# A two-layer attention and MLP training step on one core: the backward weight phases as steps with a look-ahead of two, the K4 rows loaded late, and weight-gradient stores moved to another queue

## The chip, the cores and the metric

One core of one Trainium2 chip runs the whole program. The metric is the device time of one execution in microseconds (us). The kernel before was run five times; its median is 1452.07 us, and all times lie between 1444.59 and 1456.94 us.

## The reference

The program computes a decode step of two layers, each used twice with the same weights, and all gradients:

```python
x = x + A(layernorm(x))   # attention over a K/V cache: B=2, 32 heads, 4 kv heads, Sk=16384, Dh=128
x = x + B(layernorm(x))   # layernorm again, w1 (1024x3584), gelu, w2 (3584x1024)
x = x + A(layernorm(x))
x = x + B(layernorm(x))
# outputs: x, and the gradients of A_x, k_cache, v_cache, wq, wo, w1, b1, w2, b2 for grad_out
```

There is one query row for each of two batch elements. The large arrays are the caches K and V (33.5 MB each, bf16), their gradients of the same size, and four weight matrices of 7 to 8 MB with their gradients. The gradients of K and V and of the weights sum over both uses of the layers.

## The kernel before, in words

The work runs in stages, one after the other, in one program that a tile scheduler orders for each engine. An engine then works strictly in that order.

**Forward** (`attn_fwd`, `mlp_fwd`, twice). K and V are streamed in tiles of 2 MB (`st`, a pool `stream` of six buffers that also serves all weights and the gradient tiles `stV`, `stK`). All loads are issued by SyncE (SP).

**Backward weight phases.** The gradient of a row vector through a weight matrix W needs W transposed. Three such phases form a chain: w2 (L580 transposes, L593 matmuls into `dh_acc`), the derivative of gelu, w1 (L647, L659, `dz_acc`), two layernorm derivatives (`ln_bwd_cols`, L473 to L485), wo (L698, L709, `do_acc`). After the attention pass comes wq (L886, L898, `dy_acc`). Each is a loop of steps: up to 16 transposes of 128x128 into two PSUM tiles `tp` (four slots), an eviction by ScalarE (L147) and one by VectorE (L149) into the pool `ktp` (four buffers), and four matmuls. `Skew` issues the transposes of step k+1 ahead of the matmuls of step k. The bank with the sums is copied by ScalarE (L529, L539), transposed on TensorE (L532, L542), and leads to the vector of the next phase. w1, wq and wo do this twice, for two halves, each half with a `Skew` of its own.

**Rows for the weight gradients.** Each weight gradient is a sum of four outer products. Their vectors are kept as rows of one tile `K4`, with rows 32j to 32j+3 for weight j. `k4_fill_T` transposes a vector, copies it, and writes it to K4 by two GpSimd DMAs (L519). `save_rows4` does so for the gradient at the start of a phase: eight transposes (L492), a ScalarE copy `r_bf` (L494), two DMAs (L524).

**Rows for attention** (`attn_bwd_pre`, L717 on): for each batch element three f32 transposes, a copy to SBUF (L726), a GpSimd DMA that moves the 32 rows to the partitions where they are used (L728), and then a product with its row sum (L730) and eight masked copies (L733, L734).

**Passes over the cache** (`bwd_pass`). Each has 16 units (2 batch elements by 8). A unit loads a V tile and a K tile, transposes V (L804), multiplies (`sc`, L816), forms `DS` (L820), transposes it (L838) into `DST`, and adds to `dq_ps` (L847), this last part one unit late. The first pass does only this and is called the half pass here. The second, the full pass, also makes the V gradient (`blkV`, L780) and the K gradient (`blkK`, L788), which ScalarE and VectorE evict (L758, L760) into `stV` and `stK`, stored by GpSimd. In between, `fill` takes blocks of a generator `wgrad_gen`: one block is one matmul of 512 columns with 32 rows of K4 (L972, `wgblk`) and one eviction (L138 or L140) into a tile `wg_st` of four blocks (a pool of three). Full tiles are stored in turn by GpSimd and by SP (L980). The full pass has 16 x (8+3) = 176 places for blocks, and w2, w1 and wo have 56 + 56 + 64 = 176 blocks.

**The tail**: wq with its 64 weight-gradient blocks and the small outputs. There, two ScalarE copies `ob` and `rb` (L494) come last.

The order of the stages: forward, chain 1 (w2, w1, wo), half pass, chain 2 (wq, w2, w1, wo), full pass, tail.

Of the kernel before, what the change touches and what calls it, by code (L numbers as in the profile page):

```python
# [9 lines left out]
BF16 = mybir.dt.bfloat16  # L10
# [39 lines left out]

class KB:
    def __init__(self, ctx, tc, aps, debug=None):
# [30 lines left out]
        self.ktp = self.es_main.enter_context(tc.tile_pool(name="ktp", bufs=4))  # L83
# [328 lines left out]
    def mlp_fwd(self, l, x_in):  # L412
# [25 lines left out]
        sq = self.small.tile([P, FT, NB], F32, name="g_sq")  # L438
        nc.vector.tensor_tensor(out=sq[:], in0=hp[:], in1=hp[:], op=ALU.mult)
        inner = self.small.tile([P, FT, NB], F32, name="g_inner")  # L440
        nc.vector.tensor_scalar(inner[:], sq[:], GA, 1.0, op0=ALU.mult, op1=ALU.add)
        arg = self.small.tile([P, FT, NB], F32, name="g_arg")
# [3 lines left out]
        hh = self.small.tile([P, FT, NB], F32, name="g_hh")  # L446
# [40 lines left out]

    def cols_to_rows_bf(self, colsT_bf, name):
# [4 lines left out]
        r = self.small.tile([NB, D], BF16, name=name, tag="rowbf2", bufs=2)  # L493
# [5 lines left out]
    def k4_slot(self, w, which, l, b):  # L499
        j, na, nb = self.K4_LAYOUT[w]  # L500
        r = 32 * j + 2 * l + b
        if which == "A":
            return self.K4[r:r + 1, 0:na]
        return self.K4[r:r + 1, na:na + nb]

    def k4_fill_T(self, w, which, l, src_cols, n2, blk):
        nc = self.nc
        ps = self.tp_tile([n2, P], BF16, name="k4ps")
        nc.tensor.transpose(ps[:], src_cols, self.ident[:])
        sb = self.small.tile([64, P], BF16, name="k4sb")  # L510
# [10 lines left out]
    def save_rows4(self, w, which, l, colsT_bf):  # L521
        r = self.cols_to_rows_bf(colsT_bf, "r4_bf")
# [3 lines left out]
    def extract_streams(self, acc_bank, nblk, dst_fn, name):  # L526
        nc = self.nc
        asb = self.kt_tile([P, 512], name=name + "_sb")
# [7 lines left out]
    def extract_sum(self, acc_bank, dst, name):  # L536
        nc = self.nc
        asb = self.kt_tile([P, 512], name=name + "_sb")
# [6 lines left out]
    def mlp_bwd(self, l, S, dxT, reuse_w2=False):  # L545
        nc = self.nc
        W = self.W
        dmT = self.small.tile([P, 8, NB], BF16, name="dmT")
        nc.vector.tensor_copy(dmT[:], dxT[:])
        self.save_rows4("w2", "B", l, dmT)  # L550
        if l == 1:
            nc.vector.tensor_copy(W["dxsum"][:], dxT[:])
        else:
            nc.vector.tensor_tensor(out=W["dxsum"][:], in0=W["dxsum"][:], in1=dxT[:], op=ALU.add)
        dhT = self.small.tile([P, FT, NB], F32, name="dhT")
        CH = 7
        wts = []
        for q in range(4):
            if reuse_w2:
                wts.append(S["w2tiles"][q])  # L560
            else:
                wt = self.stream_tile([P, CH, D])
                nc.sync.dma_start(wt[:], self.w2_v[:, q * CH:(q + 1) * CH, :])
                wts.append(wt)
# [526 lines left out]
```

## Time and profile before

| | |
|---|---|
| median of five runs | 1452.07 us |
| the profiled execution | 1456.94 us, of which the span is 1455.2 us |
| mean granted TensorE clock | 0.878 |
| TensorE busy | 1154.6 us (79%) |
| VectorE, ScalarE, GpSimd busy | 690.0, 553.5, 70.2 us |
| bytes moved by DMA | 488.01 MB, mean 335 GB/s |

The profile is taken from one execution. Its page gives the busy time of the engines, a row of 40 slices, the queues, the chain that ended last and the costliest groups; further views of the trace give each instruction with its start, its length and, in brackets, the idle time of its engine ahead of it with what ended that. L numbers are lines of the kernel before. "SPq" is SyncE's queue of DMA issues.

### The profile page before, as it was taken

The page shows a single profiled execution, that of the slowest core. Times are in us where ns is not written, and L with a number is a line of the kernel's source. Part 1 is how long each engine was busy: PE and PEld are TensorE (multiplying, and loading weights), DVE is VectorE, ACT ScalarE, POOL GpSimd, SP SyncE. Part 2 cuts the span into 40 slices and gives each one's busy share as a digit, 9 for nine tenths or more (in the row PEclk, how much of TensorE's full clock was granted, in tenths as well). Part 3 has the DMA queues.
Part 4 walks back from the last instruction along what each step waited for, and adds up shares of the span by engine and source line. Part 5 has one row for each costly group of instructions (what it writes and reads, how often), then busy time and mean ns, then how long its engine had stood idle before and what let it go on. Part 6 is the DMA issues. An engine that isn't in the chain of part 4 may idle for free. (4 is left out here: it accounts for less than half of the span.)

```text
span 1455.2 us, 32908 instructions
## 1 busy us (share of the span) xinstructions
PE 1154.6 (79%) x14512; PEld 699.0 (48%) x14576; DVE 690.0 (47%) x1242; ACT 553.5 (38%) x930; POOL 70.2 (5%) x120
## 2 busy tenths in 40 slices
PE   3998556589963678769987878779989999989685
PEld 2665433356653346546655556554444444433243
DVE  2566002145530224445544443457766767666553
ACT  1454000045520005422211125436657666666455
POOL 1000000000000000000000000001101001101000
PEclk9999767789975779889998888899999999998866
DMA  9998999997899983958998773917999999999963
GB/s 379 408 355 322 389 396 405 412 398 301 316 346 406 404 309 141 336 215 331 379 368 319 303 271 143 373 62 295 419 386 409 390 411 396 376 413 352 390 241 149
DMA packets 127817, 488.01 MB, mean 335 GB/s; under 512 B 5362, under 2 KB 5616, under 8 KB 122554
## 3 DMA queue, kind: packets, MB, share of 16 engines
q1 hardware_dynamic: 105642, 402.17, 71.4%
q0 software_dynamic: 22032, 83.73, 14.2%
q8 instruction: 114, 1.87, 0.5%
q14 instruction: 29, 0.24, 0.0%
HBM read 386.94 MB, written 98.58 MB: 334 GB/s over the span
## 5 line engine op out<-in xcount | busy, mean ns | idle before, releaser
L804 PE MATMUL tp<-ident,st 128*128 128x128 bf16 x2048 | 172.1, 229 | 23.0 <-DVE rows L726 13.2
L804 PEld LDWEIGHTS <-st 128*128 128x128 bf16 x2048 | 137.5, 103 | 80.0 <-issue 42.9
L246 PEld LDWEIGHTS <-st 128*128 128x128 bf16 x2048 | 119.4, 100 | 75.5 <-issue 60.7
L246 PE MATMUL tp<-ident,st 128*128 128x128 bf16 x2048 | 143.9, 224 | 12.4 <-DMA st<-in_A_k_cache_dram 12.1
L147 ACT COPY vT<-tp 128x512 f32<-128x512 f32 x128 | 75.3, 588 | 202.7 <-PE tp L804 202.6
L816 PE MATMUL sc<-vT,DOPB 128*128 128x512 bf16 x448 | 142.8, 389 | 5.8 <-DVE DS L820 3.9
L149 DVE COPY vT<-tp 128x1024 bf16<-128x1024 bf16 x128 | 88.3, 690 | 115.5 <-PE tp L804 114.1
L147 ACT COPY kT<-tp 128x512 f32<-128x512 f32 x128 | 74.8, 584 | 170.4 <-PE tp L246 169.4
L149 DVE COPY kT<-tp 128x1024 bf16<-128x1024 bf16 x128 | 87.6, 689 | 92.0 <-PE tp L246 91.0
L758 ACT CAST stV<-blkV 128x512 bf16<-128x512 f32 x160 | 92.2, 589 | 49.5 <-PE blkV L780 48.0
L788 PE MATMUL blkK<-QRP,DS 128*128 128x512 bf16 x256 | 87.0, 404 | 24.2 <-ACT stK L758 9.7
L327 PE MATMUL osc<-st,PT 128*8 128x128 bf16 x2048 | 54.4, 293 | 62.5 <-DMA st<-in_A_v_cache_dram 46.4
L758 ACT CAST stK<-blkK 128x512 bf16<-128x512 f32 x160 | 88.8, 587 | 39.8 <-PE blkK L788 39.8
L140 DVE CAST wg_st<-wgblk 128x512 bf16<-128x512 f32 x120 | 82.1, 687 | 37.1 <-PE wgblk L972 32.6
L820 DVE SCALAR_TENSOR_TENSOR DS<-sc,delta,PALL 64x1024 bf16<-64x1024 f32 (+1 forms) x64 | 82.3, 1286 | 33.6 <-PE sc L816 33.6
L972 PE MATMUL wgblk<-K 32*128 32x512 bf16 x240 | 92.8, 423 | 5.9 <-ACT wg_st L138 4.5
L261 PE MATMUL sc<-kT,QP 128*32 128x512 bf16 x512 | 88.0, 388 | 5.9 <-ACT kT L147 3.5
L760 DVE CAST stK<-blkK 128x512 bf16<-128x512 f32 x96 | 65.2, 690 | 44.6 <-PE blkK L788 44.2
L780 PE MATMUL blkV<-DORP,PALL 128*128 128x512 bf16 x256 | 84.1, 385 | 1.8 <-issue 0.2
L138 ACT CAST wg_st<-wgblk 128x512 bf16<-128x512 f32 x120 | 70.3, 589 | 36.4 <-PE wgblk L972 22.3
L327 PEld LDWEIGHTS <-PT 128*8 128x8 bf16 x2048 | 48.9, 118 | 66.9 <-issue 66.2
L847 PE MATMUL dq_ps<-st,DST 128*8 128x128 bf16 x2048 | 69.0, 227 | 6.3 <-DVE DST L149 5.1
(259 smaller groups left out, 1330.0 us busy)
## 6 DMA issues: line engine op xcount, KB each, us to landing
st<-in_A_k_cache_dram SPq DMA_DIRECT2D x64, 2048.0 KB, 16.3
st<-in_A_v_cache_dram SPq DMA_DIRECT2D x64, 2048.0 KB, 12.1
st<-in_B_w_dram SPq DMA_DIRECT2D x28, 1792.0 KB, 18.2
st<-in_A_wq_dram SPq DMA_DIRECT2D x16, 2048.0 KB, 11.7
st<-in_A_wo_dram SPq DMA_DIRECT2D x16, 2048.0 KB, 19.9
out_dram<-stV POOLq DMA_DIRECT2D x16, 2048.0 KB, 16.0
out_dram<-stK POOLq DMA_DIRECT2D x16, 2048.0 KB, 16.0
out_dram<-wg_st POOLq DMA_DIRECT2D x23, 512.0 KB, 10.9
```

The lines of the kernel that those rows point to most:

```text
L147: nc.scalar.copy(o.bitcast(F32), i.bitcast(F32))
L149: nc.vector.tensor_copy(o, i)
L246: nc.tensor.transpose(tp[:, gi, tt, :], kts[b][:, 2 * gp + gi, 4 * tg + tt, :], self.ident[:])
L261: nc.tensor.matmul(sc2[RB:RB + 32, tgi, :], lhsT=QP[:, b, g, :], rhs=kTs[b][:, gi, :, :], start=(g == 0), stop=(g == G - 1), tile_position ...
L327: nc.tensor.matmul(osc[32 * g:32 * g + 8, b, 0:DH], lhsT=PT[:, t, 32 * b + 8 * g:32 * b + 8 * g + 8], rhs=vts[b][:, g, t, :], start=(u == ...
L758: nc.scalar.copy(out, in_)
L780: nc.tensor.matmul(blk[:, :], lhsT=self.PALL[:, c0:c0 + P], rhs=W["DORP"][:, b, :, :], start=True, stop=True)
L788: nc.tensor.matmul(blk[:, :], lhsT=DS[:, t_ * P:(t_ + 1) * P], rhs=W["QRP"][:, b, :, :], start=True, stop=True)
L804: nc.tensor.transpose(tp[:, gi, tt, :], vt[:, 2 * gp + gi, 4 * tg + tt, :], self.ident[:])
L816: nc.tensor.matmul(sc2[:, tgi, :], lhsT=DOPB[:, b, g, :], rhs=vT[:, gi, :, :], start=(g == 0), stop=(g == G - 1))
L820: nc.vector.scalar_tensor_tensor(DS[ra, m * 1024:(m + 1) * 1024], sc2[ra, :, :].rearrange("p a b -> p (a b)"), W["delta"][ra, 0:1], self.P ...
L972: nc.tensor.matmul(blk[:, :], lhsT=self.K4[32 * j:32 * j + 32, ib * P:(ib + 1) * P], rhs=self.K4[32 * j:32 * j + 32, na + cg:na + cg + 512 ...
```

## The change

1. Each backward weight phase becomes an object `Phase`, with `prologue` (its loads and the transposes of the first two steps), `run` (transposes of step k+2 ahead of the matmuls of step k) and `epilogue` (the sums out). `run_bwd_chain` strings phases together: the prologue of the next phase is issued ahead of the epilogue of this one. The two halves of w1, wq and wo are one sequence of steps. The pool `ktp` has six buffers instead of four. The copies of the sums have a tile of their own, `xsb`, with one buffer.
2. The two layernorm derivatives after w1 become one function, `ln2_bwd_cols`, with one reduction over the partitions instead of two.
3. `save_rows4` and `k4_fill_T` only note what is to be written (the first copies a 128x16 vector). `k4_load` writes all rows of one weight when its blocks begin. K4 is allocated and zeroed late, all weights use rows 0 to 3, and a block multiplies all 128 rows. After each load the generator gives away 12 places (4 for wq) without a block.
4. `attn_rows` casts to bf16 and transposes straight to the partitions where the rows are used; the copy and the DMA in between are gone.
5. In the full pass the sums into `dq_ps` come in the same unit.
6. Every second weight-gradient store is issued by ScalarE instead of SP.
7. Several small tiles have one buffer, among them the tile of `ob` and `rb`.

```diff
-        self.ktp = self.es_main.enter_context(tc.tile_pool(name="ktp", bufs=4))
+        self.ktp = self.es_main.enter_context(tc.tile_pool(name="ktp", bufs=6))
...
+class Phase:
...
+    def prologue(self, n):
+        for f in self.pre:
+            f()
+        self.n = max(1, min(n, len(self.steps)))
+        for k in range(self.n):
+            self.steps[k][0]()
+
+    def run(self):
+        n = self.n
+        assert n >= 1
+        for k in range(len(self.steps)):
+            if k + n < len(self.steps):
+                self.steps[k + n][0]()
+            self.steps[k][1]()
...
+        def finish(ph):
+            ph.run()
+            start(nxt[id(ph)])
+            ph.epilogue()
...
+    def save_rows4(self, w, which, l, colsT_bf):
+        keep = self.persist.tile([P, 8, NB], BF16, name=f"k4keep_{w}{l}")
+        self.nc.vector.tensor_copy(keep[:], colsT_bf[:])
+        self.k4_src.setdefault(w, []).append(("R", w, which, l, keep))
...
-        r = self.small.tile([NB, D], BF16, name=name, tag="rowbf2", bufs=2)
+        r = self.small.tile([NB, D], BF16, name=name, tag="rowbf2", bufs=1)
...
-            ps = self.tp_tile([32, 3, DH], F32, name="rows_ps")
-            nc.tensor.transpose(ps[:, 0, :], dOT[:, :, b], self.identf[:])
...
-            r0 = self.small.tile([32, 3, DH], F32, name="rows0", bufs=1)
-            nc.vector.tensor_copy(r0[:], ps[:])
+            ps = self.tp_tile([P, 3, DH], BF16, name="rows_ps")
+            for k in range(3):
+                nc.tensor.transpose(ps[rs, k, :], srcb[:, k, b, :], self.ident[:], tile_position=(0, RB))
             rows = self.small.tile([P, 3, DH], F32, name="rowsRB", bufs=1)
-            nc.gpsimd.dma_start(rows[rs, :, :], r0[:])
+            nc.vector.tensor_copy(rows[rs, :, :], ps[rs, :, :])
...
-                pend["dq"] = dq_fn
                 if mode == 4:
+                    dq_fn()
...
+            self.k4_load(w)
+            for _ in range(idle_after_load):
+                yield
...
-                        nc.tensor.matmul(blk[:, :], lhsT=self.K4[32 * j:32 * j + 32, ib * P:(ib + 1) * P],
-                                         rhs=self.K4[32 * j:32 * j + 32, na + cg:na + cg + 512],
-                                         start=True, stop=True, tile_position=(32 * j, 0))
+                        nc.tensor.matmul(blk[:, :], lhsT=self.K4[:, ib * P:(ib + 1) * P],
+                                         rhs=self.K4[:, na + cg:na + cg + 512], start=True, stop=True)
...
-                (nc.gpsimd if qctr[0] % 2 == 0 else nc.sync).dma_start(dst, src)
+                (nc.gpsimd if qctr[0] % 2 == 0 else nc.scalar).dma_start(dst, src)
```

What the scheduler makes of it, at three places. First ScalarE in chain 1, from the last copy of w1's sums to wo; `dz_acc` and `do_acc` are the banks of w1 and wo, `w1T` (now `dzT`) and `woT` the evicted transposes. Before:

```order
L147 COPY w1T<-tp 128x512 x7
L539 CAST dz_sb<-dz_acc 128x512
L494 COPY r_bf<-c2r_ps 2x8x128
L147 COPY woT<-tp 128x512 x8
L529 CAST do_sb<-do_acc 128x512
```

And now:

```order
L175 COPY dzT<-tp 128x512 x7
L612 CAST xsb<-dz_acc 128x512
L175 COPY woT<-tp 128x512 x9
L602 CAST xsb<-do_acc 128x512
L175 COPY woT<-tp 128x512 x7
```

The copy `r_bf` between the sums of w1 and the first transposes of wo is gone, and the first half of wo is left one eviction later, since the second half has begun.

Second TensorE in the seventh unit of the half pass, around the transposes of `DS` (tiles with their buffer numbers, the same `DS` tile in all rows of a fence). Before, the seam ahead of the first eight transposes and the one between the two groups of eight:

```order
L847 MATMUL dq_ps_9162<-st_10082,DST_10273 8x128
L838 LDWEIGHTS DS_10275
...
L838 MATMUL tp_10452<-ident_82,DS_10275 128x32
L804 LDWEIGHTS st_10472
```

And now, the seam between the two groups and the one behind the second:

```order
L957 MATMUL tp_10370<-ident_82,DS_10193 128x32
L935 LDWEIGHTS DOPB3_9066
L935 MATMUL sc2_10274<-vT_10299,DOPB3_9066 128x512
...
L957 MATMUL tp_10370<-ident_82,DS_10193 128x32
L966 LDWEIGHTS DST_10387
L966 MATMUL dq_ps_9080<-st_10196,DST_10387 8x128
```

The sums into `dq_ps` of the unit before stood ahead of the transposes of `DS`, and next V's transposes behind; now the sums stand behind, and use the `DST` that has just been made. Units 2 to 8 have the first form before, units 2 to 5 now; units 9 and 11 to 16 have the second form in both.

Third ScalarE at the end of the full pass, from the last K blocks on (`dyT`, before `wqT`, are transposes of wq). Before:

```order
L758 CAST stK<-blkK 128x4x128 x10
L138 CAST wg_st<-wgblk 128x512
L147 COPY wqT<-tp 128x512 x8
L539 CAST dy_sb<-dy_acc 128x512
L138 CAST wg_st<-wgblk 128x512 x27
```

And now:

```order
L877 CAST stK<-blkK 128x4x128 x10
L166 CAST wg_st<-wgblk 128x512 x4
L1136 DMA out_dram<-wg_st 128x2x1024
L166 CAST wg_st<-wgblk 128x512 x3
L1136 DMA out_dram<-wg_st 128x2x1024
L166 CAST wg_st<-wgblk 128x512 x5
```

Between the last K block and the first transposes of wq, 39 blocks of the gradient of wo now stand in a row on TensorE; before there were 3.

More of the change, by code (lines that the diff above doesn't have):

```diff
@@ L500, in k4_slot @@
         j, na, nb = self.K4_LAYOUT[w]
[L501 removed]
+        r = 2 * l + b
         if which == "A":
@@ new lines, in epi, with dst_fn @@
+        def epi():
+            dhT = self.small.tile([P, FT, NB], F32, name="dhT")
+            acc = st["acc"]
+            accf = acc[:, :, :].rearrange("p a c -> p (a c)")
+            for half in range(2):
+                f0, nf = (0, 4) if half == 0 else (4, 3)
+                def dst_fn(k, src, f0=f0):
+                    nc.vector.tensor_copy(dhT[:, f0 + k:f0 + k + 22:7, :], src)
+                self.extract_streams(acc[:, 0, :] if half == 0 else accf[:, 512:1024], nf, dst_fn, "dh")
+            box["dhT"] = dhT
```

459 lines of the change are left out of this document (279 added, 180 removed).

## The prediction

> **What bounds the kernel now.** I first cut the execution into its stages: columns are the stretch, its length, the busy time of TensorE (PE), its weight loads, VectorE, ScalarE and GpSimd with counts, the granted TensorE clock, the DMA share and the rate.
>
> ```profile
> 0.00:538.00 538.00, 380.05 (x6137) 254.50 (x6137) 182.80 (x367) 125.03 (x216) 16.96 (x38) 0.84 0.96 375
> 538.00:642.60 104.60, 78.65 (x946) 57.86 (x947) 44.08 (x123) 41.02 (x54) 3.56 (x7) 0.86 0.63 239
> 642.60:840.00 197.40, 168.47 (x2528) 114.77 (x2559) 95.61 (x127) 37.52 (x64) 0.51 (x1) 0.92 0.83 321
> 840.00:972.70 132.70, 104.29 (x1272) 76.14 (x1273) 58.29 (x151) 51.57 (x72) 4.52 (x9) 0.87 0.60 223
> 972.70:1382.00 409.30, 369.06 (x3219) 166.67 (x3250) 273.55 (x413) 260.34 (x472) 39.83 (x56) 0.95 0.95 376
> 1382.00:1455.20 73.20, 54.05 (x412) 29.02 (x411) 35.70 (x63) 38.05 (x52) 4.79 (x9) 0.69 0.49 196
> ```
>
> The rows are forward, chain 1, half pass, chain 2, full pass, tail. Forward has its DMA engines busy for 0.96 of the time; without the K4 transposes its TensorE order is the same as before, so I leave its 538 us. The chains and the tail leave the DMA engines idle for 0.37 to 0.51 of their time: there TensorE and the waits on the way from one weight to the next set the time. The full pass has both near their limits.
>
> Then the TensorE timeline of chain 1 (start, length, what; in brackets its idle time before and what ended it).
>
> ```profile
> 540.60 1.01 PE L190 MATMUL r2c_ps<-identf,gr 2*128 2x2 f32 x8 [5.76 <-DVE gr L160]
> ...
> 555.35 1.19 PE L580 MATMUL tp<-ident,st 128*128 128x128 bf16 x16
> ...
> 557.96 1.22 PE L580 MATMUL tp<-ident,st 128*128 128x128 bf16 x16
> ...
> 568.73 0.41 PE L593 MATMUL dh_acc<-w2T,dmT 128*2 128x384 bf16 x4 [0.25 <-ACT w2T L586]
> ...
> 571.74 1.96 PE L647 MATMUL tp<-ident,st 128*128 128x128 bf16 x32
> ...
> 590.88 1.23 PE L659 MATMUL dz_acc<-w1T,dhpT 128*2 128x512 bf16 x8
> ...
> 604.68 1.02 PE L709 MATMUL do_acc<-woT,daT 128*2 128x512 bf16 x4
> ...
> 607.93 1.21 PE L698 MATMUL tp<-ident,st 128*128 128x128 bf16 x16
> ...
> 609.60 1.22 PE L698 MATMUL tp<-ident,st 128*128 128x128 bf16 x16
> ...
> 616.60 0.59 PE L709 MATMUL do_acc<-woT,daT 128*2 128x512 bf16 x3 [0.17 <-DVE woT L149]
> ...
> 642.62 1.87 PE L804 MATMUL tp<-ident,st 128*128 128x128 bf16 x16 [8.47 <-DVE rows L726]
> ```
>
> In the loops TensorE is dense: two steps of w2 take 557.96 - 555.35 = 2.61 us, one step of wo 609.60 - 607.93 = 1.67 us. The seams are not: from the end of w1 (592.11) to the first sum of wo (604.68) pass 12.6 us, and at the end of wo 8.47 us go by before the cache pass starts. Two rows say why, one of ScalarE and one of VectorE; with them two groups of the page (busy time, mean ns of one) that price an eviction of 512 columns:
>
> ```profile
> 598.88 4.80 ACT L494 COPY r_bf<-c2r_ps 2x1024 bf16<-2x1024 bf16 x1 [6.10 <-PE c2r_ps L492]
> 640.13 0.28 DVE L730 SCALAR_TENSOR_TENSOR dl_junk<-rowsRB 32x128 f32<-32x128 f32 x1 [5.72 <-DMA rowsRB<-rows]
> ```
>
> ```profile
> L140 DVE CAST wg_st<-wgblk 128x512 bf16<-128x512 f32 x120 | 82.1, 687 | 37.1 <-PE wgblk L972 32.6 <-ACT stV L758 3.7 <-PE blkV L780 0.6
> L138 ACT CAST wg_st<-wgblk 128x512 bf16<-128x512 f32 x120 | 70.3, 589 | 36.4 <-PE wgblk L972 22.3 <-DMA out_dram<-wg_st 12.9
> ```
>
> A 4.80 us copy on two partitions stands ahead of ScalarE's evictions, and VectorE waits 5.72 us for a DMA. An eviction takes 0.59 us on ScalarE and 0.69 on VectorE.
>
> **Chain 1, part by part.** Start: w2's first transposes stood behind the row copy of the gradient (`r2c_ps` is the last matmul ahead of it, and ends at 541.6); now nothing is between. Eight pairs of 2.61 make 20.9 us; with 2 us that I allow for a cold start they end at 541.6 + 22.9 = 564.5 instead of 569.1: **-4.6**. K4's clearing now stands on ScalarE ahead of the first eviction, where `r_bf` stood; the four PSUM tiles hide it, or it costs at most what that copy takes, 4.80.
>
> w1 to wo: five steps of transposes (80, by the order) now stand ahead of the first sum, where there were two. Half a phase of eight steps takes 8 x 1.67 = 13.4 us, plus 0.8 for the sums' transposes and the reduction: TensorE could end it at 592.1 + 14.2 = 606.3. The dependent chain I put at 7.3 us: the copy 0.6, 32 transposes ahead of its own 2.4, one eviction on VectorE 0.7, and some fourteen short VectorE operations, one reduction fewer than before, 3.6 at about 0.26 (the row L730 is 0.28). It ends at 599.4, after which 3 steps of transposes and 8 of sums, 8.2 us, remain: 607.6 against 617.2, **-9.6**. If the evictions hold up VectorE, up to half is lost.
>
> Attention rows: the DMA wait of 5.72 us goes; three casts come, 0.84 at 0.28. Next late is VectorE's masked copying of the first batch element, which the second's copy waits for. **-4.9**, between -3 and -5.7. Of the small seams the longest is from w2 to w1, 569.14 to 571.74, 2.6 us; with the middles of w1 and wo I take half of that and 0.75 each: **-2.8**, between 0 and -7.8. Sum **-22**.
>
> **Half pass.** Its code is the same, but the order isn't (the second place above). The loads of K on SP, one per unit, give the two paces:
>
> ```profile
> 674.02 0.37 SPq L772 DMA_DIRECT2D st<-in_A_k_cache_dram  x1
> ...
> 684.85 0.37 SPq L772 DMA_DIRECT2D st<-in_A_k_cache_dram  x1
> ...
> 778.72 0.37 SPq L772 DMA_DIRECT2D st<-in_A_k_cache_dram  x1
> ...
> 792.27 0.37 SPq L772 DMA_DIRECT2D st<-in_A_k_cache_dram  x1
> ```
>
> A unit of the first form takes 10.83 us, one of the second 13.55. Units 6, 7 and 8 change from the first to the second form: 3 x 2.72 = 8.2, and unit 10 loses some 0.8. **+9**; 0 if the transfers set the pace there, which the DMA share of 0.83 over the stage speaks against.
>
> **Chain 2.** The same rows, with wq ahead of w2:
>
> ```profile
> 843.74 3.59 PE L886 MATMUL tp<-ident,st 128*128 128x128 bf16 x32
> ...
> 868.51 1.24 PE L898 MATMUL dy_acc<-wqT,DQTb 128*2 128x512 bf16 x8
> ...
> 902.37 0.39 PE L593 MATMUL dh_acc<-w2T,dmT 128*2 128x384 bf16 x4 [0.27 <-ACT w2T L586]
> ...
> 972.70 1.86 PE L804 MATMUL tp<-ident,st 128*128 128x128 bf16 x16 [4.78 <-DVE rows L726]
> ```
>
> From the end of wq (869.75) w2 needs 20.9 + 0.8 us, and some 2 us of waits stay: 893.5 instead of 902.8, **-9.2**. w1 to wo again **-9.6**, the attention rows **-1.2** (the idle time is 4.78 here, 3.7 less than in chain 1), the first 32 transposes of wq, now ahead of the wait for their input, **-3.5**, the small seams **-2.8**. Sum **-26**.
>
> **Full pass.** SP now has only loads. Before, a store in its queue that waits for VectorE held the loads behind it:
>
> ```profile
> SPq L980 <- DVE wg_st L140: 360.9, 27, 27.8
> ```
>
> But what could earlier loads bring? The middle of the pass, from the fourth unit's first V transpose to the fifteenth's, eleven units, and the third's start:
>
> ```profile
> 1045.80:1323.10 277.30, 254.16 (x2216) 114.72 (x2239) 186.60 (x275) 179.48 (x326) 26.70 (x38) 0.96 1.01 399
> 1022.50 0.89 PE tp L804 x16
> 1045.80 1.00 PE tp L804 x16
> 1377.05 0.39 PE L788 MATMUL blkK<-QRP,DS 128*128 128x512 bf16 x1
> ```
>
> A unit without transfer waits takes 1045.8 - 1022.5 = 23.3 us, the mean is 277.3/11 = 25.2, and the DMA engines are full at 399 GB/s. So the loads there were late because the engines were full. The start and the end can gain: from 972.7 to the last K block at 1377.4 are 404.7 us. The bytes up to there, at 2.1 MB a tile and 0.13 MB a block, are 14 pairs of loads (58.7), 31 stores (65), 137 blocks (18) and two tiles of wq (4.2): 146 MB, at 400 GB/s 365 us, behind some 15 us in which the first V gradient is made. By TensorE it is 16 x 23.3 less 39 blocks moved out, 0.32 each by the two evictions side by side: 360, plus some 15 us for rows, transposes and bunched blocks after each K4 load. Both come to 375 to 380; two limits so near each other cost some more: 385, **-20** (0 to -29).
>
> [...]
>
> Widening a block from 32 to 128 rows of K4 I put at nothing: 512 columns stream either way; the DMA of the rows is covered by the 12 places given away (over a unit), or costs a landing three times, at most the 10.9 us each of the store row below.
>
> **The tail.** The 39 blocks now stand between the pass and wq:
>
> ```profile
> out_dram<-wg_st POOLq DMA_DIRECT2D x23, 512.0 KB, 10.9
> 1346.08 21.80 DMA out_dram<-wg_st
> 1395.74 12.47 PE L972 MATMUL wgblk<-K 32*128 32x512 bf16 x32
> 1413.43 0.82 PE L886 MATMUL tp<-ident,st 128*128 128x128 bf16 x6 [2.60 <-DMA st<-in_A_wq_dram]
> 1445.80 5.01 ACT L494 COPY rb<-c2r_ps 2x1024 bf16<-2x1024 bf16 x1
> ```
>
> By the evictions 39 blocks take 39 x 0.32 = 12.5 us. But they fill ten tiles of a pool of three, and a store lands 10.9 us after its issue (median; 21.80 once): about 7/3 rounds of 10.9, **25 us**. What follows shortens: wq's start is hoisted (-3.5 as in chain 2), the wait of 2.60 goes, 64 blocks can go at 0.32 instead of the 12.47/32 = 0.39 us of the row (-4.5), and with one sequence for both halves I take -5.5 of the 73.20 - 54.05 = 19 us in which TensorE idles in the tail. With one buffer, `rb` waits for the store of `ob`: `rb` ends at 1450.8, and its own store and the program's end take the 4.4 us behind it, so 0 to 4.4; I take +2.4. Net 25 - 3.5 - 2.6 - 10 + 2.4 = **+11**, between -2 and +36.
>
> **Sum.** -22 + 9 - 26 - 20 + 11 = -48. The profiled execution took 1456.94, so 1409; the median of the runs is 4.9 lower: **1404 us**.
>
> **The rivals.** (a) *The queue move brings nothing*: the full pass is set by full DMA engines throughout and stays at 404.7. For it the share of 1.01 in the middle; against it the 0.95 of the whole stage: outside the middle the share is (409.3 x 0.95 - 277.3 x 1.01)/132 = 0.82, so there is room. 1424 us.
>
> (b) *Hoisted transposes only move the wait*: VectorE has evictions between the short operations of the seam, so half of the 48 us of the chains stays. For it the one eviction in the order; against it that VectorE is busy for 44.08 of 104.60 us. 1428 us; with (a) too, 1448, no difference that can be told.
>
> (c) *Hoisted transposes run on a slow clock.* The rows at 843.74 and 571.74 price it: 32 take 3.59 us cold and 1.96 warm, so 80 take 9.0 instead of 4.9; at three long seams that is 12 us: 1416. The stretch of w1 speaks against it:
>
> ```profile
> 569.40:592.10 22.70, 20.28 (x292) 14.66 (x292) 11.59 (x27) 9.59 (x17) 1.04 (x2) 1.00 1.00 386
> ```
>
> There 224 of the 292 matmuls are transposes, and the granted clock is 1.00. [...]
>
> (d) *Slower: the stores pace the blocks.* After each K4 load the order bunches 14 to 17 blocks, four tiles, in one unit, three times, and 39 at the end. With a landing of L us, three buffers give 4L/3 per bunch and 10L/3 at the end. At the 21.80 of the row above that is 3 x (29 - 23.3) + 73 - 25 = 65 us more: 1469, slower than before. It decides from 3.33 L - 25 + 3 x (1.33 L - 23.3) = 48, at L = 19.5 us. For it that one row; against it the median of 10.9.
>
> **Chances.** Forecast 0.5, (a) 0.2, (b) 0.12, (c) 0.05, (a) with (b) 0.07, (d) 0.06. A difference of 0.5% is about what a measurement of this kernel can tell. Faster: 0.5 + 0.2 + 0.12 + 0.05 = 0.87; same 0.07; slower 0.06. The range: below, the pass at 376 and the blocks at the end at 12.5 give 1404 - 9 - 12.5, about 1382; above it reaches past (b) to 1436, and leaves out the last two cases and some of the forecast's own tails.
>
> **What would show it.** The profile after should show the first sum of wo 7 to 8 us behind the end of w1, no `r_bf` copy on ScalarE in the chains, K loads at 13.5 us from the sixth unit of the half pass on, the full pass at about 385 us, and 25 us of `wgblk` behind the last K block with ScalarE waiting for `wg_st` stores. A half pass at its old length, a full pass of 400 us, or 39 blocks in 13 us would each prove a step wrong.

## The result and the profile after

The changed kernel takes 1420.39 us (median of 9 runs), the kernel before 1454.76 us (16 runs): the ratio is 0.976, with a 95% interval from 0.974 to 0.978. 1404 us were predicted, in a range from 1382 to 1436: the direction is right, and of the 48 us that were forecast 34 came. The profiled execution of the changed kernel has a span of 1418.6 us.

First its stages, in the columns of the first fence of the prediction. The L numbers are those of the changed kernel from here on.

```profile
0.00:536.50 536.50, 377.29 (x6129) 253.53 (x6129) 181.42 (x362) 122.66 (x215) 8.24 (x22) 0.83 0.96 376
536.50:616.20 79.70, 69.46 (x927) 53.38 (x927) 43.42 (x124) 34.04 (x53) 0.00 (x0) 0.94 0.70 268
616.20:821.00 204.80, 170.06 (x2528) 117.75 (x2560) 95.55 (x127) 37.52 (x64) 0.00 (x0) 0.91 0.85 326
821.00:926.30 105.30, 94.97 (x1251) 72.01 (x1252) 56.95 (x149) 42.31 (x70) 0.00 (x0) 0.92 0.77 286
926.30:1314.80 388.50, 345.83 (x3215) 171.94 (x3250) 279.16 (x398) 248.65 (x452) 47.33 (x73) 0.96 0.94 373
1314.80:1418.60 103.80, 58.40 (x456) 28.92 (x454) 49.75 (x94) 48.55 (x72) 12.15 (x21) 0.80 0.55 222
```

The chains are far shorter, the half pass is longer, and the tail is longer by a third. To compare kernels I cut all of them at the same events of the TensorE timeline: the first matmul on the gradient (`r2c_ps`), the first V transposes of the half pass, its last sum into `dq_ps`, the first V transposes of the full pass, the end of its last K block, the end of the span. In us:

| | to chain 1 | chain 1 | half pass | chain 2 | full pass | tail |
|---|---|---|---|---|---|---|
| before | 540.6 | 102.0 | 197.2 | 132.9 | 404.7 | 77.8 |
| after | 539.1 | 77.1 | 204.7 | 105.4 | 388.5 | 103.8 |
| difference | -1.5 | -24.9 | +7.5 | -27.5 | -16.2 | +26.0 |
| forecast | 0 | -22 | +9 | -26 | -20 | +11 |

The span is 36.6 us shorter (1455.2 to 1418.6), 11.4 less than the forecast's 48. The tail alone is 15 worse than forecast, the other terms together 3.6 better. On the TensorE timeline of chain 1 the end of w1, the first and the last sums of wo, and the first transposes of the pass:

```profile
583.08 0.38 PE L724 MATMUL dz_acc<-dzT,dhpT 128*2 128x512 bf16 x2
...
590.25 1.03 PE L786 MATMUL do_acc<-woT,daT 128*2 128x512 bf16 x12 [0.31 <-DVE daT L1046]
...
608.88 1.44 PE L786 MATMUL do_acc<-woT,daT 128*2 128x512 bf16 x12
...
616.25 1.87 PE L923 MATMUL tp<-ident,st 128*128 128x128 bf16 x16 [3.80 <-DVE rowsRB L848]
```

Wo's first sum stands 6.8 us behind the end of w1 (583.46), where it was 12.6, and the wait ahead of the pass is 3.80 instead of 8.47 us. The loads of K in the half pass (SP's queue), two from its first units and two from later ones, give the two paces again, 10.76 and 13.63 us:

```profile
657.27 0.37 SPq L891 DMA_DIRECT2D st<-in_A_k_cache_dram  x1
...
668.03 0.37 SPq L891 DMA_DIRECT2D st<-in_A_k_cache_dram  x1
...
746.21 0.37 SPq L891 DMA_DIRECT2D st<-in_A_k_cache_dram  x1
...
759.84 0.37 SPq L891 DMA_DIRECT2D st<-in_A_k_cache_dram  x1
```

In the full pass SP's queue now waits for gradient tiles to land, not for VectorE to fill a store. TensorE has a new wait, for the row copies that came from the chains to VectorE (total, times, longest):

```profile
SPq L889 <- DMA out_dram<-stV: 185.3, 11, 19.8
```

```profile
PE tp L923 <- DVE r_bf L595: 12.5, 4, 3.6
```

And the tail, on TensorE, from the last K block to the first transposes of wq:

```profile
1314.43 0.39 PE L907 MATMUL blkK<-QRP,DS 128*128 128x512 bf16 x1
1314.65 1.79 PE L1129 MATMUL wgblk<-K 128*128 128x512 bf16 x5
...
1336.77 1.95 PE L1129 MATMUL wgblk<-K 128*128 128x512 bf16 x4 [15.84 <-ACT wg_st L166]
...
1352.32 1.95 PE L705 MATMUL tp<-ident,st 128*128 128x128 bf16 x32 [0.88 <-DVE wg_st L168]
```

The 39 blocks take 1351.5 - 1314.8 = 36.7 us, and 15.84 of them are one wait. TensorE waits there for ScalarE's eviction, and ScalarE for a store of four blocks to land, the one that it had issued at 1318.93; it landed some 17 us later:

```profile
1318.93 0.38 ACTq L1136 DMA_DIRECT2D out_dram<-wg_st  x1
1336.13 1.07 ACT L166 CAST wg_st<-wgblk 128x512 bf16<-128x512 f32 x2 [16.17 <-DMA out_dram<-wg_st]
```

The chain that ended last names a store that was issued a little earlier by GpSimd, landed at 1340.7 and ended the next, shorter wait:

```profile
1317.14 23.55 DMA out_dram<-wg_st
```

Until then the DMA engines are full (share 1.02), with the last tiles of the K and V gradients and the loads of wq under way beside these stores; the later stores of blocks whose landing the trace gives take 3 to 5 us.

```profile
1314.80:1340.80 26.00, 6.35 (x19) 1.75 (x17) 6.55 (x14) 4.61 (x9) 2.19 (x3) 0.65 1.02 422
```

### The profile page after: what moved, and what is told of

Same layout as the page of the kernel before. It is cut to its first block, busy times and chain, and to the rows that moved or that the text cites. A ratio compares the mean times of both kernels' runs of the same rounds, so it can differ in the third digit from the quotient of the medians.

```text
span 1418.6 us, 32828 instructions
## 1 busy us (share of the span) xinstructions
PE 1116.0 (79%) x14504; PEld 697.5 (49%) x14572; DVE 706.2 (50%) x1252; ACT 533.7 (38%) x926; POOL 67.7 (5%) x116
## 4 chain that ended last, share of the span: by engine, by line
PE 55%; DMA 24%; DVE 11%; ACT 4%; issue 4%; SPq 1%; POOL 0%; POOLq 0%; DVEq 0%; ACTq 0%
PE tp L274 9%; PE tp L923 8%; PE sc L935 7%; DMA st<-in_A_v_cache_dram 6%; DMA st<-in_A_wo_dram 6%; PE sc L289 5%; DMA out_dram<-wg_st 4%; DMA st<-in_A_k_cache_dram 4%; PE blkK L907 4%; DVE DS L939 4%; PE blkV L899 3%; PE dq_ps L966 3%; DMA st<-in_B_w_dram 3%; PE tp L645 2%; PE wgblk L1129 2%
## 5 line engine op out<-in xcount | busy, mean ns | idle before, releaser
L923 PE MATMUL tp<-ident,st 128*128 128x128 bf16 x2048 | 170.6, 231 | 25.5 <-DVE r_bf L595 12.5
L923 PEld LDWEIGHTS <-st 128*128 128x128 bf16 x2048 | 146.3, 104 | 84.6 <-issue 37.0
L274 PEld LDWEIGHTS <-st 128*128 128x128 bf16 x2048 | 118.7, 100 | 76.0 <-issue 60.7
L274 PE MATMUL tp<-ident,st 128*128 128x128 bf16 x2048 | 143.0, 223 | 13.1 <-DMA st<-in_A_k_cache_dram 12.6
L1129 PE MATMUL wgblk<-K 128*128 128x512 bf16 x239 | 84.0, 394 | 28.1 <-ACT wg_st L166 20.6
L879 DVE CAST stV<-blkV 128x512 bf16<-128x512 f32 x96 | 66.1, 689 | 12.5 <-PE blkV L899 11.6
## 6 DMA issues: line engine op xcount, KB each, us to landing
out_dram<-stV POOLq DMA_DIRECT2D x16, 2048.0 KB, 13.7
out_dram<-wg_st POOLq DMA_DIRECT2D x23, 512.0 KB, 12.6
```

What stands on the lines that cost most here:

```text
L274: nc.tensor.transpose(tp[:, gi, tt, :], kts[b][:, 2 * gp + gi, 4 * tg + tt, :], self.ident[:])
L879: nc.vector.tensor_copy(out, in_)
L923: nc.tensor.transpose(tp[:, gi, tt, :], vt[:, 2 * gp + gi, 4 * tg + tt, :], self.ident[:])
L1129: nc.tensor.matmul(blk[:, :], lhsT=self.K4[:, ib * P:(ib + 1) * P], rhs=self.K4[:, na + cg:na + cg + 512], start=True, stop=True)
```

## The experiments

Seven kernels undo one thing in the changed kernel (one of them three), one leaves stores out, three try another order, and one changes the kernel before. Their stages, cut at the same events:

| | median us | ratio to before, interval | chain 1 | half pass | chain 2 | full pass | tail |
|---|---|---|---|---|---|---|---|
| changed kernel | 1420.4 | 0.976, 0.974 to 0.978 | 77.1 | 204.7 | 105.4 | 388.5 | 103.8 |
| stores on SP | 1438.2 | 0.989, 0.987 to 0.992 | 77.3 | 205.5 | 105.4 | 400.8 | 110.0 |
| blocks back, 32 rows | 1454.6 | 1.000, 0.998 to 1.002 | 77.1 | 205.5 | 105.6 | 443.5 | 86.2 |
| no last stores (one run) | 1400.1 | | 76.7 | 205.2 | 105.4 | 389.8 | 82.8 |
| next phase late | 1428.9 | 0.983, 0.980 to 0.985 | 79.9 | 207.5 | 106.7 | 389.4 | 104.3 |
| row copy back | 1446.3 | 0.993, 0.991 to 0.996 | 91.8 | 202.1 | 118.6 | 388.7 | 104.2 |
| dq late | 1423.3 | 0.978, 0.976 to 0.980 | 76.8 | 204.7 | 105.5 | 391.4 | 104.0 |
| no places given | 1424.1 | 0.979, 0.977 to 0.981 | 77.6 | 204.7 | 105.2 | 426.1 | 70.1 |
| 32 rows | 1453.3 | 1.000, 0.998 to 1.003 | 76.3 | 204.5 | 105.5 | 409.0 | 118.3 |
| dq spread | 1420.3 | 0.979, 0.975 to 0.982 | 76.9 | 203.7 | 102.2 | 389.7 | 105.5 |
| no drain | 1417.4 | 0.976, 0.974 to 0.978 | 76.4 | 204.5 | 105.3 | 388.6 | 101.7 |
| both, copy divided | 1409.4 | 0.974, 0.970 to 0.978 | 76.7 | 206.2 | 102.6 | 386.3 | 99.4 |

**The stores back on SP.**

```diff
-                (nc.gpsimd if qctr[0] % 2 == 0 else nc.scalar).dma_start(dst, src)
+                (nc.gpsimd if qctr[0] % 2 == 0 else nc.sync).dma_start(dst, src)
```

> Part 6 alone is undone: every second store of the weight gradients is issued by SyncE again, ahead of the loads in its queue. The forecast's theory (the move of the stores gave most of what the full pass gained): the full pass grows from 388 us to about 400, 1432 us in all. The rival (a) (the queue move brings nothing; the pass is shorter because 36 blocks left it, 36 x 0.32 = 11.5 us): the pass stays within 3 us of 388, about 1420 us.

It took 1438.2 us: the full pass takes 400.8 us, 12.3 more, the tail 6.2 more. The forecast's theory holds, and its size of 400 for the pass too. SP's queue shows the old wait again, and the row of the pass (columns as in the stages) a DMA share of 0.91:

```profile
SPq L1136 <- DVE wg_st L168: 222.1, 19, 17.6
```

```profile
928.30:1329.10 400.80, 350.83 (x3246) 172.65 (x3248) 278.14 (x398) 249.46 (x452) 47.16 (x73) 0.94 0.91 358
```

What the move takes away is this wait of 222.1 us inside SP's queue. With it gone the share in the pass is 0.94, and the whole gains 18 us.

**The blocks back in the pass, in groups of 32 rows**, with the rows loaded one weight ahead.

```diff
-        r = 2 * l + b
+        r = 32 * j + 2 * l + b
...
-    def wgrad_gen(self, ws, use_wgs=True, idle_after_load=12):
+    def wgrad_gen(self, ws, use_wgs=True, idle_after_load=0):
...
+            if wi + 1 < len(ws):
+                self.k4_load(ws[wi + 1])
...
+                        nc.tensor.matmul(blk[:, :], lhsT=self.K4[32 * j:32 * j + 32, ib * P:(ib + 1) * P],
+                                         rhs=self.K4[32 * j:32 * j + 32, na + cg:na + cg + 512],
+                                         start=True, stop=True, tile_position=(32 * j, 0))
```

> K4 keeps each weight's rows in a group of 32 partitions of its own again (a block multiplies 32 rows), the rows are written one weight ahead, and no place in the pass is given away, so that about 3 blocks instead of 39 are left behind the last K block. Theory (the tail's loss is the 37 us of blocks held up by their stores, and in the pass a block costs the 0.32 us of its eviction): the pass grows by 36 x 0.32 = 11.5 us, the tail shrinks by 35, about 1397 us. Rival (the DMA engines are full to the end, and the loads of wq take the place of the stores as what the tail waits for): the tail shrinks by 12 at most, 1415 to 1420 us.

It took 1454.6 us, and neither side had it: the tail did shrink by 17.6 us, but the pass grew by 55. My price of 0.32 us for a block in the pass was wrong, or the edit had brought something else. It had changed three things: the places given away, the 32 rows and when the rows are loaded. The next two kernels test the first two alone; the third was not tried alone.

**No place given away** (`idle_after_load` 0 instead of 12, nothing else).

> As the changed kernel (blocks of 128 rows, rows loaded late), but no place in the pass is given away: 36 blocks go back into the pass, 3 are left behind it. The second experiment, which also went back to groups of 32 rows, lost 55 us in the pass. Theory A (that loss came from blocks of 32 rows in bursts at a granted clock of about 0.6): here the pass grows by 12 to 15 us, the tail shrinks by 30, about 1403 us. Theory B (it came from blocks that wait for their K4 rows right behind a load, with everything queued behind them): here too the pass grows by 40 us or more, 1430 us or more.

It took 1424.1 us: the pass grows by 37.6, the tail shrinks by 33.7. Theory B fits the pass, though the sum came out below its figure. On TensorE, a first block behind the second load:

```profile
1074.45 1.07 PE L966 MATMUL dq_ps<-st,DST 128*8 128x128 bf16 x64 [0.58 <-DVE DST L177]
1083.67 0.59 PE L1129 MATMUL wgblk<-K 128*128 128x512 bf16 x1 [8.15 <-DMA K<-k4sb]
```

It waits 8.15 us for its rows, with the V blocks queued behind it, and so the stores of the gradients. Three stretches, one behind each load, show the DMA engines idling, in the columns of the stages (in the changed kernel the 20 us that match the first have a share of 0.53, and behind the other two loads the lowest is 1.01 and 0.78):

```profile
945.50:965.50 20.00, 15.29 (x124) 6.20 (x124) 10.89 (x16) 10.59 (x20) 1.51 (x2) 0.91 0.23 88
1065.50:1105.50 40.00, 25.88 (x225) 12.54 (x227) 19.25 (x28) 17.24 (x32) 6.25 (x12) 0.87 0.78 299
1205.50:1225.50 20.00, 15.14 (x132) 7.38 (x134) 10.14 (x14) 6.85 (x13) 2.48 (x4) 0.73 0.52 203
```

So the places given away are worth 3.7 us in sum, which the two intervals don't tell from nothing: 36 blocks cost about a microsecond each on either side, in the pass with the waits for their rows in it.

**32 rows instead of 128** in a block.

```diff
-                        nc.tensor.matmul(blk[:, :], lhsT=self.K4[:, ib * P:(ib + 1) * P],
-                                         rhs=self.K4[:, na + cg:na + cg + 512], start=True, stop=True)
+                        nc.tensor.matmul(blk[:, :], lhsT=self.K4[0:32, ib * P:(ib + 1) * P],
+                                         rhs=self.K4[0:32, na + cg:na + cg + 512], start=True, stop=True, tile_position=(0, 0))
```

> One change to the changed kernel: a block multiplies 32 rows of K4 (rows 0 to 31, in which all the data is) instead of 128; the places given away, the loads and the order stay as they are. The prediction's step (widening costs and brings nothing, 512 columns stream either way): within 4 us, 1417 to 1424 us. Theory A (32 rows leave the granted clock low where blocks come in bursts): the drained blocks and those of wq run at 0.5 to 0.6 and the whole is 10 to 25 us slower, 1430 to 1445 us.

It took 1453.3 us: theory A holds, and the whole gain of the change is gone with this one line (which also sets the tile position that goes with 32 rows; the two were not separated). The pass is 20.5 us longer and the tail 14.5. The full pass and a stretch of the tail (the rest of wq with its 64 blocks) in this kernel, and the same stretch in the changed one:

```profile
925.50:1334.50 409.00, 367.97 (x3215) 165.63 (x3250) 279.55 (x398) 249.91 (x452) 47.18 (x73) 0.92 0.92 356
1389.50:1437.00 47.50, 42.68 (x183) 14.87 (x180) 26.78 (x49) 22.15 (x39) 2.17 (x4) 0.58 0.44 177
```

```profile
1368.80:1400.00 31.20, 26.00 (x160) 10.55 (x158) 24.55 (x45) 20.86 (x38) 2.18 (x4) 1.00 0.58 237
```

TensorE is busy in 42.68 of 47.50 us and is granted 0.58 of its clock; with 128 rows it is granted 1.00. In the pass the clock is 0.92 on average instead of 0.96. The second kernel of this section, which also loads its rows one weight earlier, lies 30.5 us above the one without places given: about the same loss.

**128 rows in the kernel before.** Is the wide block then simply worth 33 us?

```diff
-                        nc.tensor.matmul(blk[:, :], lhsT=self.K4[32 * j:32 * j + 32, ib * P:(ib + 1) * P],
-                                         rhs=self.K4[32 * j:32 * j + 32, na + cg:na + cg + 512],
-                                         start=True, stop=True, tile_position=(32 * j, 0))
+                        nc.tensor.matmul(blk[:, :], lhsT=self.K4[:, ib * P:(ib + 1) * P],
+                                         rhs=self.K4[:, na + cg:na + cg + 512], start=True, stop=True)
```

> The kernel before with one edit: a block multiplies all 128 rows of K4 instead of the 32 of its weight (the rows of the other weights are in the sums then, so the gradients of the weights are not those wanted; the work is otherwise the same). Theory A (blocks of 32 rows in bursts leave the granted clock at 0.5 to 0.6, and the wider blocks alone make up most of what the change gained): the stretch behind the last K block, at 0.53 to 0.67 before, runs at 0.9 or more and is 10 to 15 us shorter, the full pass some 10 to 20 us shorter, together 1420 to 1432 us. Rival (rows cost only in the changed kernel, whose blocks come in longer bursts; here they are spread out): 10 us less at most, 1443 us or more.

It took 1447.7 us, a ratio of 0.995 (0.993 to 0.998): the rival's figure. The pass gains 8.5 us (396.2), the tail 1.9 (75.9). On TensorE in the tail, with the lines of the kernel before:

```profile
1386.09 10.07 PE L972 MATMUL wgblk<-K 128*128 128x512 bf16 x31
...
1404.52 0.82 PE L886 MATMUL tp<-ident,st 128*128 128x128 bf16 x6 [6.04 <-DMA st<-in_A_wq_dram]
```

The blocks are faster, 10.07/31 = 0.32 us against 12.47/32 = 0.39, but then the second half of wq is late: the wait of 2.60 us has become 6.04, since these loads stand behind two stores that hold SP's queue for 22.99 us and are issued only at 1392.33. So behind the pass most of what the wide block gains is lost again in SP's queue; whether it would bring more in this kernel with the stores on another queue was not tried.

**The row copy back in the chains.**

```diff
         self.nc.vector.tensor_copy(keep[:], colsT_bf[:])
+        ps = self.tp_tile([NB, 8, P], BF16, name="c2r_ps")
+        for c in range(8):
+            self.nc.tensor.transpose(ps[:, c, :], colsT_bf[:, c, :], self.ident[:])
+        r = self.small.tile([NB, D], BF16, name="r_bf", tag="rowbf2", bufs=1)
+        self.nc.scalar.copy(r[:].rearrange("b (p s) -> b s p", s=8), ps[:])
```

> As the changed kernel, but at the start of w2 and of wo the eight transposes of the vector and the ScalarE copy of two partitions come back (into a tile that nobody reads), ahead of the evictions of the phase, four times in all. Theory (the seams became short because this copy of 4.8 us no longer stands ahead of the evictions): some 4 us are lost at each of the four places, 16 us, about 1436 us. Rival (the prologues ahead of the epilogues made the seams short, and hide the copy): 5 us at most, 1425 us or less.

It took 1446.3 us: the theory holds, and 26 us are lost instead of 16. The chains lose 14.7 and 13.2. The copy on ScalarE ahead of wo's evictions, and the first 9 us of wo:

```profile
595.53 4.79 ACT L570 COPY r_bf<-c2r_ps 2x1024 bf16<-2x1024 bf16 x1 [4.71 <-PE c2r_ps L568]
```

```profile
597.30:606.00 8.70, 7.64 (x65) 4.78 (x64) 2.23 (x4) 5.09 (x5) 0.00 (x0) 0.62 1.03 407
```

The seam is 9.0 us long (588.3 to 597.3) instead of 6.8. It holds 48 of wo's transposes instead of 80, since the eight transposes of the row wait for the vector and stand ahead of the rest in TensorE's order. And there is a second price that I had not asked for: wo starts at a clock of 0.62. It takes 27.5 us instead of 20.1; in the next kernel, which has as many transposes left, it takes 24.0, with 1.20 to 1.22 us for 16 transposes between its sums, about as in the changed kernel at a clock of 1.00, so about 3.5 us of the 7.4 lie in the clock and the late evictions. W2 takes 22.0 us from its first sum to its last (546.0 to 568.0) instead of 18.3 (544.9 to 563.2).

**The next phase late** (its prologue behind the epilogue).

```diff
-            start(nxt[id(ph)])
-            ph.epilogue()
+            ph.epilogue()
+            start(nxt[id(ph)])
```

> The prologue of the next phase is issued behind the epilogue of this one instead of ahead; two steps of look-ahead inside a phase, the joined halves and the later row copies stay. Theory (the transposes hoisted into the seams are what the chains gained): each of the three long seams loses about 6 us and each of the two from w2 to w1 2.4, 23 us in all, about 1443 us. Rival (b) (the hoisted transposes only move the wait): at most half of that, 1432 us or less.

It took 1428.9 us, 8.5 more: rival (b) holds, with less than half of what the theory wanted. The seam from w1 to wo on TensorE:

```profile
586.05 1.16 PE L770 MATMUL tp<-ident,st 128*128 128x128 bf16 x16
587.05 0.37 PE L524 MATMUL lnb_tot<-lnb_part,onesf 128*128 128x4 f32 x2
587.27 2.18 PE L770 MATMUL tp<-ident,st 128*128 128x128 bf16 x32
589.89 0.60 PE L786 MATMUL do_acc<-woT,daT 128*2 128x512 bf16 x4 [0.44 <-DVE daT L1046]
```

The scheduler still puts 48 of the transposes into the seam where there were 80, and the seam is even shorter (w1 ends at 585.1, so 4.8 us); probably since fewer evictions stand among VectorE's short operations. Wo then takes 24.0 us instead of 20.1. So this kernel does not take the look-ahead away, it shortens it; what a seam without any would cost was not tried.

**The sums into dq_ps late** (part 5 undone: `pend["dq"] = dq_fn` in the full pass too).

> Part 5 alone is undone: in the full pass the sums into dq_ps come one unit late again. Theory (the pass is set by the DMA engines and the evictions, these sums of TensorE only fill): within 5 us of the changed kernel, 1415 to 1425 us. Rival (part 5 is what made the pass shorter beside the queue move): 5 to 15 us slower, all in the pass.

It took 1423.3 us, with 2.9 us more in the pass: the theory holds, and part 5 is worth no more than this.

**No last stores.** This kernel leaves out the stores of the blocks made behind the pass, so part of the gradient of wo is missing.

```diff
-                (nc.gpsimd if qctr[0] % 2 == 0 else nc.scalar).dma_start(dst, src)
+                if not getattr(self, "drain", False):
+                    (nc.gpsimd if qctr[0] % 2 == 0 else nc.scalar).dma_start(dst, src)
```

> As the changed kernel, but the blocks of the gradient of wo that are made behind the pass are not stored (this leaves that part of the output out). Theory (three store buffers pace these blocks): they take 39 x 0.32 = 12.5 us instead of 37, the whole about 1396 us. Rival (the loads of wq, issued from 1300 on, land late behind the last gradient tiles anyway): TensorE then waits for wq, no more than 10 us are gained, about 1409 us.

It took 1400.1 us in its one run, 20 less: the theory holds. The transposes of wq start with no wait for their load, 16.4 us behind the last K block (1315.6) instead of 37.5:

```profile
1332.04 1.95 PE L705 MATMUL tp<-ident,st 128*128 128x128 bf16 x32 [0.88 <-DVE wg_st L168]
```

**No drain**: could the same be had with the stores?

```diff
-    kb.fill(10000)
     kb.switch_psum(tp=3, sc2=0, acc=1, blk=4)
-    kb.filler = kb.wgrad_gen(["wq"], use_wgs=False, idle_after_load=4)
+    kb.filler = itertools.chain(kb.filler, kb.wgrad_gen(["wq"], use_wgs=False, idle_after_load=4))
```

> The last 39 blocks of the gradient of wo are not made ahead of wq any more: they are made in the places between the steps of wq, the 64 blocks of wq behind them. Theory (the tail lost because wq stands behind blocks that wait for their stores; leaving the stores out brought 20 us): the steps of wq begin some 20 us earlier, and these waits lie beside them, 22 to 30 us less, about 1393 us. Rival (the tail is set by all its evictions and stores, whatever their order): 10 us less at most, 1410 us or more.

It took 1417.4 us: the rival's figure. Fifteen of the blocks are still put ahead of nearly all of wq and meet a store as late as before, and at the end the blocks of wq stand behind the two ScalarE copies `ob` and `rb` (4.68 and 4.67 us in the changed kernel):

```profile
1334.67 0.58 PE L1129 MATMUL wgblk<-K 128*128 128x512 bf16 x1 [15.72 <-ACT wg_st L166]
...
1383.61 7.09 PE L1129 MATMUL wgblk<-K 128*128 128x512 bf16 x19 [8.65 <-ACT wg_st L166]
```

More store buffers would be the direct test; it was not tried, and whether buffers alone would bring the 20 us stays open.

**The sums spread over the unit** in the half pass.

```diff
+                            if "dq" in pend:
+                                pend["dq"](t0=2 * k, t1=2 * k + 2)
...
-                def dq_fn(u=u, DST=DST, kt=kt):
-                    for t_ in range(T):
+                def dq_fn(u=u, DST=DST, kt=kt, t0=0, t1=T):
+                    for t_ in range(t0, t1):
```

> In the half pass the sums into dq_ps of the unit before are written eight at a time among the eight steps of a unit, instead of all behind them. By this the seam between the transposes of DS is filled with next transposes of V again in units 2 to 9. The prediction's step (the order of TensorE sets the pace of a unit): units 6 to 9 at least go from 13.6 us to about 10.8, 11 to 22 us less in the half pass, 1398 to 1409 us. Rival (the transfers or the evictions set the pace there, and the order only follows): the half pass stays at 205 us, about 1420 us.

It took 1420.3 us; the half pass is 1.0 us shorter. That is the rival's figure, but not its mechanism: the third and fourth units became slower, and the fifth to ninth, at 12.5 to 13.9 us in the changed kernel, faster. Two loads of K in SP's queue:

```profile
650.45 0.37 SPq L891 DMA_DIRECT2D st<-in_A_k_cache_dram  x1
662.47 0.37 SPq L891 DMA_DIRECT2D st<-in_A_k_cache_dram  x1
```

12.02 us a unit, between the 10.76 and the 13.63 of the two old forms. The pace changed with the order alone, so the order does set it; this order is a third one and not the good one.

**Both together**, with the row copy in the pass divided between VectorE and ScalarE.

```diff
-        self.nc.vector.tensor_copy(r[:].rearrange("b (p s) -> b s p", s=8), ps[:])
+        rv = r[:].rearrange("b (p s) -> b s p", s=8)
+        self.nc.vector.tensor_copy(rv[:, 0:4, :], ps[:, 0:4, :])
+        self.nc.scalar.copy(rv[:, 4:8, :], ps[:, 4:8, :])
```

> The two changes above together, and the row copy of two partitions in the full pass is divided between VectorE and ScalarE, four chunks each. If the theories of the two hold, their gains add, and the divided copy takes off half of the 12.5 us in which TensorE waits for it: 1420 - 16 - 25 - 6, about 1373 us. If their rivals hold, 1410 us or more.

It took 1409.4 us, near the rivals' figure and far from 1373. It is the lowest median of the kernels that store every gradient, but two of its six runs took 1425 us and the intervals of the two ratios overlap, so that it beats the changed kernel is not shown. The wait for the row copy went from 12.5 to 10.5 us only:

```profile
PE tp L925 <- ACT r_bf L597: 10.5, 4, 3.8
```

## Why the prediction was right, point by point

- **Chain 1** (-22, measured -24.9). By its terms: the start from 28.5 us (540.6 to 569.1) to 24.1 (539.1 to 563.2), -4.4 for -4.6 (the first 44 transposes now run at a granted clock of 0.56 and take 4.55 us, where at 1.96 for 32 they would take 2.7: near the 2 us allowed for a cold start); from w1's end to wo's last sum 39.5 to 26.8, -12.7 for -9.6 (a term that went to the end of wo's first half only); the rows from 11.0 to 5.9 (wo's last sum to the pass), -5.1 for -4.9. What I had not counted is the clock. In the kernel before, the seam had 0.69 and wo's next 12.3 us 0.90; both stretches are at 1.00 now, so wo's own steps are faster:

```profile
592.10:604.70 12.60, 5.87 (x52) 4.96 (x52) 4.28 (x21) 6.29 (x4) 0.72 (x2) 0.69 1.04 394
604.70:617.00 12.30, 12.13 (x129) 7.83 (x128) 4.84 (x7) 3.52 (x6) 0.27 (x1) 0.90 0.64 230
```

The cause was half right. I credited the transposes ahead of the first sum; the experiments give 14.7 + 13.2 = 27.9 of the chains' 52.4 us to the row copy taken out, and 2.8 + 1.3 = 4.1 to the place of the prologue, as far as that kernel moved it. The joined halves, the single reduction and the new rows for attention were not undone, so the other 20 us are not divided.
- **Half pass** (+9, measured +7.5): the two forms of a unit take 10.76 and 13.63 us, as read from the trace of before; the fifth and sixth units, at 12.9 and 12.5 us, lie between them.
- **Chain 2** (-26, measured -27.5): the sum came out by luck, since terms that were missed balance. The start of wq brought 0.6 us instead of 3.5 (its first sum comes 6.9 us behind the half pass instead of 7.5): the transposes still wait for the copy `DQSB`, and run at a granted clock of 0.50.

```profile
822.36 3.57 PE L705 MATMUL tp<-ident,st 128*128 128x128 bf16 x32 [1.39 <-DVE DQSB L978]
```

From wq's end to w2's last sum 33.0 us became 27.0, -6.0 for -9.2. Against that stand w1's end to wo's last sum with -12.9 for -9.6, the rows with -2.0 for -1.2, and the small seams and joined halves, wq from its first sum on (-3.4) and w2's last sum to w1's (-2.7), with -6.1 for -2.8.
- **Full pass** (-20, measured -16.2). The queue move does what the forecast said (12.3 us), so rival (a) is out. The sum was reached for partly wrong reasons, so that it came close is partly luck: leaving 36 blocks out I priced at 0.32 us each, and it is about a microsecond each with the waits for their rows; against that stand the rows, transposes and bunched blocks, for which I had some 15 us, and of which the row copies alone make TensorE wait 12.5.
- **128 rows** ("I put at nothing"): the step that failed outright, and hidden by the sum. The median block does take as long either way, 385 ns over 32 rows in the kernel before and 379 over 128 in the changed one, but the granted clock differs. If the blocks were 32 rows wide, the clock would be 0.58 in the stretch with wq's 64 blocks and 0.92 on average in the pass, and the whole 33 us longer. I had the row that said so: the 12.47 us for 32 blocks, 0.39 each where the evictions allow 0.32. I read it as an eviction that could be faster, and did not ask why TensorE was busy throughout in a stage with a clock of 0.69.
- **The tail** (+11, measured +26): the mis-sized step. The 39 blocks were put at 25 us, with the median landing of 10.9; they took 36.7. At that place the landing is not the median: the first three stores take 17 to 23.55 us, with the engines full. Rival (d) had the row of 21.80 and the right place, but counted 3.33 rounds of it there, and one came; of its price in the pass nothing came, where ScalarE and VectorE wait 1.0 us together for such stores. The rest, wq to the end, shrank by 77.8 - 1.2 - (1418.6 - 1351.5) = 9.5 us (the last blocks before take 1.2), where I had 13.7.
- **Rival (c)**, transposes on a slow clock: refuted, as the stretch of w1 said. Its two rows stand at granted clocks of 0.50 (843.74) and 1.00 (571.74). But in the seam from 583.5 to 590.2 nearly all of the 85 matmuls are transposes, and the granted clock is 1.00:

```profile
583.50:590.20 6.70, 5.84 (x85) 5.46 (x85) 4.71 (x20) 2.35 (x4) 0.00 (x0) 1.00 1.05 385
```

- **Rival (b)** has the right observation (the place of the prologue alone is worth little) and the wrong total, since something else shortened the seams.

The parts do not add up: undone one at a time, 128 rows, the row copies, the queue and the prologue are worth 33.0 + 26.0 + 17.9 + 8.5 = 85 us, and the change brought 34. Part of the rest pays for what the change itself costs: the tail, the half pass, the copies in the pass. And 128 rows alone in the kernel before bring 6.5. So what a part is worth depends on the others, and these figures are no account that adds up.

## What to carry to other kernels

Read the granted clock beside the busy time of TensorE wherever a stretch is full of one kind of matmul: here a busy engine at 0.58 was worth 33 us for one line, and a term "the same columns stream" does not see it. When work is moved out of a seam, price it again where it lands, with the duration of a transfer at that place and not the median. Where an edit is undone to test it, undo it alone: the kernel that undid three at once could not be read until two of them were tested alone.

## What the runs showed of the hardware that I had not expected

- Matmuls of 128 columns by 512 over 32 rows left the granted clock at 0.58 over a stretch while TensorE was busy for nine tenths of the time (42.68 of 47.50 us); over 128 rows, of which 124 are zero, it was 1.00 with TensorE busy for 26.00 of 31.20 us. So being busy in the profile's sense was not enough there for the full clock.
- Two seams and the stretch behind a third: a seam of 12.6 us in the kernel before, with TensorE busy for 5.87 of them, had a granted clock of 0.69, the one of 6.7 us in the changed kernel, busy for 5.84, had 1.00, and the first 8.7 us of wo behind the seam of 9.0 us in the kernel with the row copy 0.62.
- A copy of 2x1024 elements on two partitions costs about the same on either engine, 4.79 us on ScalarE, and on VectorE two in a row 9.21:

```profile
932.41 9.21 DVE L595 COPY r_bf<-c2r_ps 2x1024 bf16<-2x1024 bf16 x2
```
